# Attention and routed experts in one kernel: where some VectorE copies, two groups of ranking products, and the stores of eight pairs of output rows are placed

## The chip, the cores and the metric

The kernel runs on one core of a Trainium2 chip. The metric is the device time of one execution in microseconds; the time before is the median of three runs. The engines are named as in the profile: PE (TensorE, with PEld for its weight loads), DVE (VectorE), ACT (ScalarE), POOL (GpSimd) and SP (SyncE, which here only issues DMAs). Each engine carries out its own instructions in the order of the program; engines wait for each other by semaphores.

## What is computed

Linear attention without a softmax, a normalization of each head's rows, and on the result a layer of eight experts of which each row uses one:

```python
q, k, v: (8, 8, 576, 64)                       # batch, heads, rows, head dim
kv  = einsum('bhsd,bhse->bhde', k, v)
out = einsum('bhsd,bhde->bhse', q, kv)
x   = out / sqrt(mean(out*out, -1) + 1e-6) * g_norm     # then (4608, 512): heads side by side
compute = x @ w_skip > 0                       # the other rows are returned as they are
logits  = x @ w_gate                           # 8 experts
e       = argmax(logits);  gate = softmax(logits)[e]
y       = gate * (relu(x @ w1[e]) @ w2[e])     # w1: (8, 512, 1024), w2: (8, 1024, 512)
out     = x + y
```

## The kernel before

All matrices are 32-bit floats. The order of all work is written out by hand: the program is one schedule, and what stands earlier in it for an engine runs earlier on that engine.

**Attention** goes over 36 *units*. A batch has 9 rows for each of 64 partitions; a *pair* `nq` is a tile `xb` of 128 partitions by 2 rows by 512 columns (512 KB) of final x, and two units (four heads each, `u` = 0 and 1) make one pair. Every batch has two pairs (`i` = 0, 1: eight of its nine rows), and after each four batches comes one pair with the ninth rows (`i` is None). So pairs 0 to 7 are of batches 0 to 3, pair 8 their ninth rows, 9 to 16 of batches 4 to 7, pair 17 the rest. `starts[b]` is the first unit of batch b: 0, 4, 8, 12, 18, 22, 26, 30; units 16 and 17 are pair 8, units 34 and 35 pair 17.

For a batch, `state` (L383) sums k^T v in PSUM (`sum_ps`), ScalarE copies it to SBUF (`both`, L390), and from there it goes into a block matrix `kvd`: DVE copies the halves that change partitions (`other`, L394), POOL those that stay (`own`, L395). `state_t` (L400) transposes it, and `state_m` (L408) multiplies the router's weights into it, whose result ScalarE copies into the 9 columns at the ends of `kvd` by four small copies (L412). `kvT_ps`, the router's products and the rank table lie in one PSUM bank, the tile `g_ps`. A batch's `state` work is cut into pieces and put into the steps of the batch before (`portions`).

**Steps.** The schedule's main loop has one step for each unit n. On PE and ACT a step holds, in this order: `turn(n+1)`, the transposes of q (L460) and the copy `qT` (L463, ACT); the square root of unit n-1 (L529, ACT); jobs of the part "early"; `values(n)`, the products q·kvd (L498, or L508 for ninth rows) in one of two PSUM buffers, with the ninth rows' transposes (L479) in the first units of a batch, and the squares on ACT (L514); jobs of "mid"; on DVE the sums of squares (L522) and the normalization of unit n-1 (reciprocal L536, `xl` L545, which sets the PSUM buffer free); jobs of "pe"; POOL's sums of logits (L597 to L605); and jobs of "end". POOL multiplies by g_norm one step later (`xb`, L615), held back until DVE's reciprocal.

**Gating** has three groups (`ends = [12, 22, 36]`). For the first two, a generator hands DVE a few small instructions at the end of each step (2 a step for group 0, 4 for group 1): the chosen expert by maximum and comparison (`choose`, L665 to L685, one-hot `ohb`), then `rank` on PE (L696, L699, L702), which counts the rows in front of each row for its expert, then `number` on DVE. `rank` runs in step 16 for group 0 and in step 24 for group 1, in the part "pe", behind the `state_m` that runs in the same step. Behind group 1 the experts are sorted by their number of rows, SP reads the order into registers and loads the first expert's `w1` (L337, step 26). From the known rows (batches 0 to 4) the first expert's first rows are then looked up (`early`, L899 to L915, with PE's L924) and gathered from the output in DRAM by POOL (L917, step 30). PE turns them at L848 in step 33, and the first layer on them starts at L859.

**DMA.** SP issues all loads of q, k and v (L118; k and v have three buffers, q two, and the load of batch b + 2 of q stands at the end of step `starts[b] + 2`), the weights, and most stores of x. A finished pair is stored by two halves of 256 KB: at the end of the step that follows its last multiplication on POOL, not before `store_from` (step 24 for pairs 8 and 9). For pairs with i = 1 of batches 0 to 6, POOL issues the first half itself (L649), SP the second (L653). `xb` has six buffers. The pool `wpool_a` holds one expert's `w1` and `w2`; the room of `w2` is used from the start for the router's rows, a few constants and a block of zeros (`room`), the room of `w1` stands empty until L337. `load_second` loads `w2` in step 32.

**Filling products.** `dense` issues products of a constant with itself, 128x512 in bf16 (L171), whose result nobody reads; they stand where PE would wait at the start, and once near the end of attention.

Behind the attention come the eight experts, one by one, with weights in two pools in turn (L1172, L1184, L1252 on PE; results scattered by POOL at L1383).

Of the kernel before, what the change touches and what calls it, by code (L numbers as in the profile page):

```python
# [8 lines left out]
FP32 = mybir.dt.float32  # L9
# [8 lines left out]
def kernel(  # L18
# [43 lines left out]
    nc = tc.nc  # L62
    B, H, S, D = q.shape
    DM = H * D
    N = B * S
    P = 128
# [6 lines left out]
    E, F = moe_w1.shape[0], moe_w1.shape[2]  # L73
    G = E + 1
    KD = D + G
    DC = DM // 128
# [71 lines left out]

    room = wpool_a.tile([P, FC, DM], FP32, tag="w2", name="w2")
    room = room[:, :, :].rearrange("p c d -> p (c d)")  # L150
    wrow = room[0:4, 0:P * E].rearrange("p (q n) -> p q n", n=E)
    nc.scalar.dma_start(out=wrow, in_=moe_w_gate.rearrange("(j q) n -> j q n", q=P))
    srow4 = room[0:4, P * E:P * G]
# [11 lines left out]

    warm_ps = ps_q.tile([P, 512], FP32, tag="q", name="q_ps")

    def dense(count, ps=warm_ps):

        for _ in range(count):  # L170
            nc.tensor.matmul(out=ps[:, :], lhsT=ones[:, :],  # L171
                             rhs=ones[:, :].unsqueeze(1).to_broadcast([P, 4, P]), start=True, stop=True)

    dense(11)

# [39 lines left out]
    for n in range(G):  # L215
# [3 lines left out]
    gcol_ps = set_ps[:, 1, 0:1]  # L219
    nc.tensor.transpose(out=gcol_ps, in_=room[0:1, P * G:P * G + 2 * D],  # L220
                        identity=ident[0:1, 0:1])
    dense(2)
    gcol = setup.tile([P, 1], FP32)
    nc.scalar.copy(out=gcol[:, :], in_=gcol_ps)
    gbig = room[:, P * G + P:P * G + 2 * P]
# [125 lines left out]
            tc.add_manual_dep(ins.ins, behind.ins.name, WAIT, reason="gathers first")  # L351


    kvTs, boths = {}, {}

    def own(b, w):

# [2 lines left out]
    def other(b, w):  # L360

        return kvds[b % KVD][(1 - w) * 64:(2 - w) * 64, w, 1 - w, :, :]
# [12 lines left out]
    def state(b, some):  # L375

        kt, vt = kts[b], vts[b]
        for i in some:
            u, c = divmod(i, C)
            for w in range(2):  # L380
                for a in range(2):
                    r = slice(a * 64, (a + 1) * 64)
                    nc.tensor.matmul(  # L383
                        out=sum_ps[w * 64:(w + 1) * 64, a, u, :],
                        lhsT=kt[r, 2 * u + w, c, :], rhs=vt[r, 2 * u + w, c, :],
                        start=(c == 0), stop=(c == C - 1), skip_group_check=True)
        if some.stop < 2 * C:
            return
        both = att_pool.tile([P, 2, 2 * D], FP32, tag="both", name="both", bufs=1)
        nc.scalar.copy(out=both[:, :, :].rearrange("p u (a d) -> p a u d", a=2), in_=sum_ps)  # L390
        boths[b] = both
        cols = slice(G, G + 2 * D)
        for w in range(2):
            nc.vector.tensor_copy(out=other(b, w)[:, :, cols], in_=both[w * 64:(w + 1) * 64, :, :])  # L394
            nc.gpsimd.tensor_copy(out=own(b, w)[:, :, cols], in_=both[w * 64:(w + 1) * 64, :, :])  # L395

    def state_t(b):
        both = boths.pop(b)
        for u in range(2):
            nc.tensor.transpose(out=kvT_ps[:, u, :], in_=both[:, u, :], identity=ident[:, :])  # L400
        kvT = att_pool.tile([P, 2, P], FP32, tag="kvT", name="kvT", bufs=1)
        nc.scalar.copy(out=kvT[:, :, :], in_=kvT_ps)
        kvTs[b] = kvT

    def state_m(b):
        kvT = kvTs.pop(b)
        for u in range(2):
            nc.tensor.matmul(out=lg_ps[:, u, :, :, :], lhsT=kvT[:, u, :], rhs=gw_b[:, u, :, :, :],  # L408
                             start=True, stop=True)
        for w in range(2):  # L410
            for to in (own, other):
                nc.scalar.copy(out=ends_of(to(b, w)), in_=lg_ps[w * 64:(w + 1) * 64, :, :, w, :])  # L412


    units = []
    nq = 0
# [25 lines left out]
    def at(step, part, job):  # L442
        todo.setdefault((step, part), []).append(job)
# [165 lines left out]
    def weigh(n, xl):  # L609

        nq, b, i, u = units[n]
        if u == 0:
            xbs[nq] = xb_pool.tile([P, 2, DM], FP32, tag="xb", name="xb")
        xb = xbs[nq]
        late.append((lambda eng: eng.tensor_tensor(  # L615
            out=xb[:, :, 4 * u * D:(4 * u + 4) * D].rearrange("p r (w x) -> p r w x", w=2),
            in0=xl[:, :, :, G:G + 2 * D] if i is None else
            xl[:, :, :, G:G + 2 * D].rearrange("p w r x -> p r w x"),
            in1=g_b[:, :, :].rearrange("p a d -> p (a d)").unsqueeze(1).unsqueeze(1)
                .to_broadcast([P, 2, 2, 2 * D]), op=ALU.mult), nq, u == 1 and (lambda: store_x(nq, b, i))))  # L620

    store_from = {x[0]: starts[B - 3] + 2 for x in units if x[1:3] in ((0, None), (4, 0))}

    def scale(n, behind=None, keep=0, eng=None):

# [9 lines left out]
    def store_x(nq, b, i):  # L635

        xb = xbs.pop(nq)
        if i is None:
            rows = out.rearrange("(f hf r p c) d -> f hf p r c d", f=NF, hf=2, r=2, c=C)[b]
            def store():  # L640
                for hf in range(2):
                    nc.sync.dma_start(out=rows[hf, :, :, C - 1, :], in_=xb[hf * 64:(hf + 1) * 64, :, :])
            return store
        rows = out[b * S:(b + 1) * S, :].rearrange("(p c) d -> p c d", c=C)[:, 4 * i:4 * i + 4, :]
        rows = rows.rearrange("p (hf r) d -> hf p (r d)", hf=2)
        x = xb[:, :, :].rearrange("p r d -> p (r d)")
        first = int(i == 1 and b < B - 1)
        if first:
            nc.gpsimd.dma_start(out=rows[0], in_=x[0:64, :])  # L649

        def store():
            for hf in range(first, 2):
                nc.sync.dma_start(out=rows[hf], in_=x[hf * 64:(hf + 1) * 64, :])  # L653
        return store
# [295 lines left out]
            in_=zero)  # L950

    state(0, range(C))
    dense(4)
    state(0, range(C, 2 * C))
    dense(2)
    state_t(0)
    turn(0)
    state_m(0)
# [5 lines left out]
    for b, n in starts.items():  # L964
        if b:
            step, counts = portions[b]
            i = 0
            for count in counts:
                at(step, "early" if step in (starts[2], starts[4] - 2) else "pe",
                   lambda b=b, some=range(i, i + count): state(b, some))  # L970
                i += count
                step += 1
            assert i == 2 * C and step < n and step - len(counts) > over - 1
            at(step, "early", lambda b=b: state_t(b))
            at(step, "pe", lambda b=b: state_m(b))
            over = step
        at(over, "end", lambda b=b: load_kv(b + 3, range(4 if b > 1 else 2)))

        at(n + 2, "end", lambda b=b: load_q(b + 2))
        if b < 2:  # L980
            at(n + 2, "end", lambda b=b: load_kv(b + 3, range(2, 4)))

    def gating(g):

        yield from choose(g)
        yield lambda: rank(g)
        numbers = number(g)
        yield next(numbers)
        if g == LAST - 1:
            yield from rank_experts()  # L990
            load_weights(0, wpool_a, later=True)
        yield from numbers
        if g == LAST - 1:
            yield from early()
# [633 lines left out]
```

## Time and profile before

| | |
|---|---|
| runs | 366.98, 367.38, 367.67 us; median 367.38 |
| profiled execution | 366.29 us, of which the span of instructions 364.4 us |
| granted PE clock, mean | 0.994 |
| busy | PE 349.5, PEld 305.5, DVE 249.2, ACT 145.1, POOL 125.7 us |
| moved by DMA | 81.70 MB, mean 224 GB/s |

In the profile, times are microseconds from the first instruction. "PE g_ps L696 x2" is two instructions of line 696 that write the tile g_ps; what stands in brackets behind an instruction is how long its engine was idle before it, and what ended the wait. The chain is followed back from the last instruction, at each step to what released it. A float32 product appears as two passes, so 16 products of L508 are 32 instructions.

### The profile page before, as it was taken

Reading aid. Unit: us, or ns where it says so; the run is one execution under the profiler, and the core shown is the slowest. Engines: PE = TensorE matmul, PEld = TensorE weight load, DVE = VectorE, ACT = ScalarE, POOL = GpSimd, SP = SyncE. Lnnn points to the kernel's source line nnn. Section 1 sums busy time; section 2 is a strip of 40 time slices with the busy share of each in tenths; the row PEclk is TensorE's granted clock in tenths of the full one; section 3 lists DMA queues with packets and bytes.
Section 4 is the critical chain, followed back from the end, with each engine's and each line's share of the span. In section 5 each row is a group of like instructions: output and inputs, shape, how many; then the busy total and the mean of one; then the engine's idle time right before and its main releaser. Section 6 shows DMA issues by size and latency. Waiting matters only on the chain.

```text
span 364.4 us, 9568 instructions
## 1 busy us (share of the span) xinstructions
PE 349.5 (96%) x3754; PEld 305.5 (84%) x3754; DVE 249.2 (68%) x637; ACT 145.1 (40%) x418; POOL 125.7 (34%) x205
## 2 busy tenths in 40 slices
PE   8979998999899999999999999999999999999994
PEld 4769987888779669599879978989988998989983
DVE  2545677889888563876937676786776776878831
ACT  2537775676666244244104402512421530431420
POOL 8036777677776072123041102303203203002003
PEclk9989999999999999999999999999999999999999
DMA  8999999999797369873535537455563762601001
GB/s 272 387 390 377 371 392 398 394 394 384 247 335 255 104 208 379 340 262 89 209 107 205 171 124 254 121 224 176 175 230 98 250 235 53 243 1 58 3 2 54
DMA packets 32808, 81.70 MB, mean 224 GB/s; under 512 B 3242, under 2 KB 3250, under 8 KB 32756
## 3 DMA queue, kind: packets, MB, share of 16 engines
q1 hardware_dynamic: 28944, 69.48, 53.7%
q0 software_dynamic: 3792, 11.53, 9.3%
q8 instruction: 31, 0.51, 0.5%
q14 instruction: 21, 0.17, 0.1%
q10 hardware_dynamic: 20, 0.02, 0.0%
HBM read 66.80 MB, written 14.48 MB: 223 GB/s over the span
## 4 chain that ended last, share of the span: by engine, by line
PE 79%; issue 6%; DMA 5%; DVE 5%; POOL 2%; ACT 2%; SPq 0%; POOLq 0%; DVEq 0%; ACTq 0%
PE bank L1252 46%; PE bank L1184 9%; PE o_ps L498 6%; PE sum_ps L383 4%; PE bank L1172 3%; PE q_ps L460 3%; DMA v<-in_v_dram 2%; PE bank L1153 2%; DVE xl L545 1%; DMA xg<-out_dram,src 1%; PE g_ps L859 1%; DMA xg<-out_dram,asrc 1%; PE q_ps L859 1%; PE o_ps L479 1%; DVE rs L522 1%
## 5 line engine op out<-in xcount | busy, mean ns | idle before, releaser
L1262 ACT COPY p<-bank 128x128 f32<-128x128 f32 (+6 forms) x70 | 20.8, 297 | 96.1 <-PE bank L1252 94.6
L1252 PE MATMUL bank<-xt,w 128*128 128x128 f32 (+5 forms) x336 | 55.4, 288 | 0.1
L1383 POOL DMA_INDIRECT out_dram<-xg,rows x14 | 13.9, 996 | 116.2 <-DVE xg L1380 113.0
L1252 PEld LDWEIGHTS bank<-xt,w 128*128 128x128 f32 x336 | 47.0, 190 | 1.9 <-DVE bank L1256 1.4
L615 POOL TENSOR_TENSOR xb<-xl,g_b 128x512 f32<-128x512 f32 x34 | 41.3, 1216 | 18.1 <-DVE rs L536 16.1
L1256 DVE TENSOR_TENSOR bank<-bank,p 128x128 f32<-128x128 f32 (+6 forms) x70 | 23.6, 337 | 29.7 <-PE bank L1252 28.7
L498 PE MATMUL o_ps<-kvd,qT 128*128 128x146 f32 x240 | 36.0, 293 | 1.3 <-DVE xl L545 1.0
L1252 PE MATMUL bank<-xs,s 128*128 128x128 f32 (+5 forms) x224 | 36.7, 288 | 0.0
L498 PEld LDWEIGHTS o_ps<-kvd,qT 128*128 128x128 f32 x240 | 32.1, 192 | 2.1 <-DVE xl L545 1.8
L1252 PEld LDWEIGHTS bank<-xs,s 128*128 128x128 f32 x224 | 31.1, 190 | 1.0 <-ACT p L1262 0.8
L1184 PE MATMUL bank<-w,ht 128*32 128x128 f32 (+2 forms) x424 | 29.9, 313 | 0.0
L522 DVE TENSOR_REDUCE rs<-sq 128x8 f32<-128x512 f32 x36 | 24.5, 681 | 5.4 <-ACT sq L514 5.2
L545 DVE TENSOR_TENSOR xl<-o_ps,rs 128x584 f32<-128x584 f32 x32 | 24.5, 767 | 4.3 <-DVE rs L536 0.5
L1184 PEld LDWEIGHTS bank<-w,ht 128*32 128x32 f32 (+2 forms) x424 | 18.2, 119 | 10.6 <-issue 7.2
L1252 PE MATMUL bank<-t,ht 128*128 128x256 f32 x112 | 27.0, 384 | 0.0
L1252 PE MATMUL bank<-w,ht 128*128 128x256 f32 x112 | 26.5, 380 | 0.0
L383 PE MATMUL sum_ps<-v,k 64*64 64x64 f32 x1152 | 23.5, 223 | 3.0 <-issue 2.6
L1144 POOL DMA_INDIRECT xg<-out_dram,src x14 | 14.3, 1024 | 34.8 <-DMA out_dram<-xg,rows 18.0
L514 ACT ACTIVATE sq<-o_ps 128x512 f32<-128x512 f32 x34 | 20.3, 596 | 14.1 <-PE o_ps L498 13.2
L383 PEld LDWEIGHTS sum_ps<-v,k 64*64 64x64 f32 x1152 | 19.6, 134 | 7.1 <-issue 3.9
L1252 PE MATMUL bank<-t,hs 128*128 128x256 f32 x112 | 25.3, 379 | 0.0
L1252 PEld LDWEIGHTS bank<-t,ht 128*128 128x128 f32 x112 | 20.8, 190 | 3.9 <-issue 1.2
(216 smaller groups left out, 665.2 us busy)
## 6 DMA issues: line engine op xcount, KB each, us to landing
w<-in_moe_w_dram SPq DMA_DIRECT2D x16, 2048.0 KB, 9.0
k<-in_k_dram SPq DMA_DIRECT2D x32, 288.0 KB, 6.0
v<-in_v_dram SPq DMA_DIRECT2D x32, 288.0 KB, 6.3
q<-in_q_dram SPq DMA_DIRECT2D x32, 288.0 KB, 6.2
out_dram<-xb SPq DMA_DIRECT2D x29, 256.0 KB, 6.1
out_dram<-xb POOLq DMA_DIRECT2D x7, 256.0 KB, 6.4
xg<-out_dram,src POOLq DMA_INDIRECT x16, 3.6
out_dram<-xg,rows POOLq DMA_INDIRECT x16, 6.1
```

The source lines that it names most:

```text
L383: nc.tensor.matmul(out=sum_ps[w * 64:(w + 1) * 64, a, u, :], lhsT=kt[r, 2 * u + w, c, :], rhs=vt[r, 2 * u + w, c, :], start=(c == 0), stop ...
L498: mm = nc.tensor.matmul(out=ps[:, w, 0:2 * PK].rearrange("p (r k) -> p r k", r=2)[:, :, cols], lhsT=qT[:, w, a, :], rhs=kvds[b % KVD][:, w ...
L514: nc.scalar.activation(out=sq[:, :, :, :], in_=heads(ps, G, G + 2 * D), func=ACT.Square)
L522: nc.vector.tensor_reduce(out=rs[:, :, :], in_=sq[:, :, :, :].rearrange("p x y (a d) -> p x (y a) d", a=2), axis=AX.X, op=ALU.add)
L545: nc.vector.tensor_tensor(out=xl[:, :, :, :].rearrange("p x y (a k) -> p x (y a) k", a=2), in0=ps[:, :, 0:2 * PK].rearrange("p x (h k) -> ...
L615: late.append((lambda eng: eng.tensor_tensor(out=xb[:, :, 4 * u * D:(4 * u + 4) * D].rearrange("p r (w x) -> p r w x", w=2), in0=xl[:, :, ...
L1144: nc.gpsimd.indirect_dma_start(out=x_of(xg, off, m), out_offset=None, in_=cut_rows(m)[:, :], in_offset=bass.IndirectOffsetOnAxis(ap=idx[:, ...
L1184: nc.tensor.matmul(out=yps[q * m:(q + 1) * m, 0:n], lhsT=ht(f)[:, off:off + m], rhs=w_sb[r][1][:, f, q * n:(q + 1) * n], start=(f == 0), s ...
L1252: nc.tensor.matmul(out=out, lhsT=lhsT(i), rhs=rhs(i), start=start and i == 0, stop=i == k - 1, skip_group_check=True)
L1256: nc.vector.tensor_tensor(out=to, in0=x, in1=y, op=ALU.add)
L1262: nc.scalar.copy(out=t, in_=x)
L1383: ins = nc.gpsimd.indirect_dma_start(out=cut_rows(m)[:, :], out_offset=bass.IndirectOffsetOnAxis(ap=rows[:, col:col + 1], axis=0), in_=x, ...
```

## The change

- `held` takes the empty room of the first expert's `w1`. Pairs 2 to 5 of x are written into it, pairs 6 to 9 into the room of its `w2`; pairs 0, 1 and from 10 on use the buffers of `xb`.
- Pairs 0 to 10 are stored from given steps on: 2 and 3 from step 20, 4 and 5 from 21, 6 from 22, 0, 1, 7, 8 and 9 from 24 (behind the load of q of batch 7, which stands at the end of the same step), 10 from 25. Both halves of these are issued by SP, so five of POOL's seven issues (L649) are gone.
- For batches 5, 6 and 7 the two copies to `other` are made by ScalarE in the step before the batch's first unit (steps 21, 25 and 29), in "mid", that is behind that step's squares.
- `rank` of groups 0 and 1 moves from "pe" to "mid": on PE it comes right behind the step's `values`, ahead of `state_m` and of the piece of `state` in "pe".
- Three runs of filling products at the start are issued as four times as many of 128 columns.

```diff
+    held = wpool_a.tile([P, DC, F], FP32, tag="w1", name="w1")
+    held = held[:, :, :].rearrange("p c f -> p (c f)")
...
-    def dense(count, ps=warm_ps):
-
-        for _ in range(count):
-            nc.tensor.matmul(out=ps[:, :], lhsT=ones[:, :],
-                             rhs=ones[:, :].unsqueeze(1).to_broadcast([P, 4, P]), start=True, stop=True)
+    def dense(count, ps=warm_ps, cut=1):
+
+        for _ in range(count * cut):
+            nc.tensor.matmul(out=ps[:, 0:512 // cut], lhsT=ones[:, :],
+                             rhs=ones[:, :].unsqueeze(1).to_broadcast([P, 4 // cut, P]),
+                             start=True, stop=True)
...
-    dense(2)
+    dense(2, cut=4)
...
-    kvTs, boths = {}, {}
+    kvTs, boths, ACROSS = {}, {}, 5
...
         for w in range(2):
-            nc.vector.tensor_copy(out=other(b, w)[:, :, cols], in_=both[w * 64:(w + 1) * 64, :, :])
+            if b < ACROSS:
+                nc.vector.tensor_copy(out=other(b, w)[:, :, cols], in_=both[w * 64:(w + 1) * 64, :, :])
             nc.gpsimd.tensor_copy(out=own(b, w)[:, :, cols], in_=both[w * 64:(w + 1) * 64, :, :])
 
+    def state_across(b):
+        if b < ACROSS:
+            return
+        both = boths.pop(b)
+        for w in range(2):
+            nc.scalar.copy(out=other(b, w)[:, :, G:G + 2 * D], in_=both[w * 64:(w + 1) * 64, :, :])
+
     def state_t(b):
-        both = boths.pop(b)
+        both = boths[b]
...
         if u == 0:
-            xbs[nq] = xb_pool.tile([P, 2, DM], FP32, tag="xb", name="xb")
+            home = nq - ROOMS_FROM
+            if 0 <= home < 8:
+                x = (held, room)[home // 4][:, home % 4 * 2 * DM:(home % 4 + 1) * 2 * DM]
+                xbs[nq] = x.rearrange("p (r d) -> p r d", r=2)
+            else:
+                xbs[nq] = xb_pool.tile([P, 2, DM], FP32, tag="xb", name="xb")
...
-    store_from = {x[0]: starts[B - 3] + 2 for x in units if x[1:3] in ((0, None), (4, 0))}
+    ROOMS_FROM = 2
+    at_q7 = starts[B - 2] - 2
+    store_from = {0: at_q7, 1: at_q7, 2: at_q7 - 4, 3: at_q7 - 4, 4: at_q7 - 3, 5: at_q7 - 3,
+                  6: at_q7 - 2, 7: at_q7, 8: at_q7, 9: at_q7, 10: at_q7 + 1}
...
-        first = int(i == 1 and b < B - 1)
+        first = int(i == 1 and b < B - 1 and nq not in store_from)
...
     state(0, range(C))
-    dense(4)
+    dense(4, cut=4)
     state(0, range(C, 2 * C))
-    dense(2)
+    dense(2, cut=4)
...
             at(step, "pe", lambda b=b: state_m(b))
+            at(n - 1, "mid", lambda b=b: state_across(b))
...
         yield from choose(g)
-        yield lambda: rank(g)
+        yield "mid", lambda: rank(g)
```

## The prediction

> **What bounds the kernel now.** I read the page first, then the busy time of each engine in stretches of ten microseconds, the chain of work that ended last, the timelines of PE, DVE, ACT and SP around the lines of the diff, and last the DMA. All edits act before 107 us; what follows (the experts) is PE work end to end, so I take a shift of the first gathered rows as a shift of the end.
>
> ```profile
> span 364.4 us, 9568 instructions
> ...
> PE   8979998999899999999999999999999999999994
> ```
>
> ```profile
> 70.00:80.00 10.00, 10.00 (x188) 8.95 (x182) 8.42 (x20) 6.93 (x20) 6.95 (x14) 1.00 1.03 392
> 80.00:90.00 10.00, 9.34 (x203) 8.43 (x204) 9.15 (x28) 6.62 (x18) 6.91 (x12) 1.00 1.04 383
> 90.00:100.00 10.00, 8.33 (x108) 7.51 (x107) 8.99 (x25) 6.56 (x20) 7.85 (x16) 1.00 0.76 261
> ```
>
> The columns are the stretch, its length, then busy time of PE, PEld, DVE, ACT and POOL, the granted clock, the DMA share and GB/s. From 70 to 80 us PE has no gap: attention runs at PE's pace. From 80 to 100 PE loses 0.66 + 1.67 = 2.3 us while DVE is 18.1 of 20 us busy: there the second gating group's work is threaded between the units on DVE, and DVE sets the pace. DMA is full until 90 us. The chain names the two places where the ranking products sit, and the road to the first gather:
>
> ```profile
> 61.81 0.20 ACT kvd L412
> 62.05 0.47 PE g_ps L696 x2
> 62.57 0.34 PE g_ps L702 x12
> 62.90 0.51 PE q_ps L460 x4
> 63.44 0.58 ACT qT L463
> ...
> 65.38 0.41 PE o_ps L479 x2
> ...
> 82.01 0.29 DVE kvd L394
> 82.33 0.41 DVE kvd L394
> ...
> 83.13 0.49 DVE ohb L685
> ...
> 84.40 0.46 PE g_ps L696 x2
> ...
> 85.14 0.49 PE q_ps L460 x4
> ...
> 93.04 0.29 DVE kvd L394
> 93.36 0.37 DVE kvd L394
> ...
> 99.75 0.71 PE g_ps L924 x22
> ...
> 101.37 5.18 DMA xg<-out_dram,src
> 106.69 0.63 PE q_ps L848 x4
> ```
>
> Start, length, and what. The first product of `rank` (L696) starts right behind ScalarE's small copies out of the same PSUM bank (61.81 + 0.20, then 62.05). Two pairs of `kvd` copies on DVE (L394) lie on the chain. The gather lands 0.14 us before PE uses it (101.37 + 5.18 = 106.55), so whatever brings the gather forward brings the rest forward only if PE, too, comes earlier; both hang on the same DVE chain.
>
> **The change part by part.** *Ranks first, group 0 (step 16).* The unit's products run before L408; the order of PE there is
>
> ```profile
> 59.84 0.69 PE L508 MATMUL o_ps<-kvd,q 64*64 64x73 f32 x32
> 60.46 0.64 PE L408 MATMUL g_ps<-gw_b,kvT 128*128 128x36 f32 x4
> ```
>
> and the one-hot that `rank` reads is done before that:
>
> ```profile
> 60.23 0.27 DVE L685 TENSOR_TENSOR ohb<-eorder,fi 128x96 bf16<-128x96 f32 x1
> ```
>
> So in "mid", ahead of L408, `rank` waits for nothing: it starts at about 60.6 and lasts as now, 62.90 - 62.05 = 0.85, to 61.45; L408's 0.45 follows to 61.9, and PE's next transposes start at 61.9 instead of 62.90, 1.0 earlier. But ScalarE's four copies (0.8 in all, they start when L408 has ended) now run 61.95 to 62.75 and stand ahead of the qT copy, which so moves from 63.44 to 62.8. From there the chain above is kept: qT, root, reciprocal, xl, and PE's L479 at 64.75 instead of 65.38. **-0.6**, between 0 (the wait turns up behind L412 again) and -1.0 (all that PE gains).
>
> *Ranks first and the copies of batch 6 (step 24).* Here the one-hot is late: it ends at 83.62, while the unit's products end at 82.79:
>
> ```profile
> 81.80 1.16 PE L498 MATMUL o_ps<-kvd,qT 128*128 128x146 f32 x8
> 82.79 0.53 PE L408 MATMUL g_ps<-gw_b,kvT 128*128 128x36 f32 x4
> 83.25 0.69 PE L383 MATMUL sum_ps<-v,k 64*64 64x64 f32 x32
> ```
>
> The edit alone would make PE wait in front of L408 and L383, which stand behind it: 83.65 + 0.74 (rank, 85.14 - 84.40) + 0.46 + 0.62 = 85.47, 0.3 later than 85.14. But the DVE copies of batch 6 (82.01 to 82.74) go to ScalarE, so the one-hot ends near 82.9, and PE comes out at 82.95 + 1.82 = 84.77. **-0.4**, between +0.3 (one-hot no earlier) and -0.6 (no wait left).
>
> *The copies of batch 7 (step 28).* DVE has 0.72 us less to do at 93.04 (start of the first copy to 93.76, the next instruction), with no idle time of its own behind it until the gather's index is built. PE waits for DVE there:
>
> ```profile
> 96.19 1.26 PE L498 MATMUL o_ps<-kvd,qT 128*128 128x146 f32 x8 [1.02 <-DVE xl L545]
> 97.29 0.60 PE L460 MATMUL q_ps<-ident,q 128*128 128x128 f32 x4
> ...
> 97.94 1.16 PE L498 MATMUL sum_ps<-kvd,qT 128*128 128x146 f32 x8
> 99.75 0.69 PE L924 MATMUL g_ps<-bv,oha_k 128*128 128x4 bf16 x22 [0.65 <-DVE bv L904]
> ```
>
> Taken from 96.19 and from 99.75, both DVE's: **-0.7**, between 0 and -1.0 (the whole wait). The copies of batch 5 lie where PE is full, between 70 and 80: 0.
>
> *What ScalarE takes over.* Two copies of 64x256 for each of batches 5 to 7, in steps 21, 25 and 29, right before the unit that reads them. The trace has no such copy from SBUF; the nearest rows are
>
> ```profile
> 81.09 0.37 ACT L390 COPY both<-sum_ps 128x256 f32<-128x256 f32 x1
> 97.55 0.60 ACT L514 ACTIVATE sq<-o_ps 128x512 f32<-128x512 f32 x1 [0.48 <-PE o_ps L498]
> ```
>
> 0.37 each, 0.74 the pair. They stand behind the squares (0.60, of which I take 0.5, since the next instruction overlaps its end), so the next unit's products can start 1.25 to 1.3 after the last ones end. In steps 21 and 25 PE has a piece of state (0.62, as at 83.25) and transposes (97.94 - 97.29 = 0.65) in between, 1.27: just covered. What waits on ScalarE is the next qT copy and the root behind it, some 0.1 late in step 21, where they lead to the gating group's first maximum: **+0.1**. In step 29 only the 0.65 lies between, so unit 30 starts 0.6 late; but L924, behind it on PE, has 0.65 of slack. If the units move up by 1.1 (0.4 + 0.7), unit 30 ends near 98.5 and L924's operand comes at 98.6: nothing lost. Without that cover: up to +0.6. The Trainium skill ("ScalarE: Activation LUTs", Rules for kernel authors) speaks against such a move: simple element work belongs on VectorE. In this trace DVE's copies have no better price:
>
> ```profile
> L394 DVE COPY kvd<-both x16: 286/372/452, 12.5 to 93.4; 64x256 f32<-64x256 f32 x16
> ```
>
> median 372 ns against 372 for L390, and from 80 to 100 us ACT is two thirds busy where DVE is nine tenths. By that page's own price (186 ns + 0.833 an element, an estimate of 399 ns) the pair would be 0.80 and the sum 0.1 worse.
>
> *Stores.* Pairs 0 to 10 (0.52 MB each, as the page's 256 KB a half says) are no longer stored as they come but from step 20 on, wholly by SP. SP's queue now:
>
> ```profile
> 78.02 6.06 SPq L118 DMA_DIRECT2D q<-in_q_dram  x8
> ...
> 92.71 0.42 SPq L337 DMA_DIRECT2D w<-in_moe_w_dram  x1
> ```
>
> ```profile
> 90.00:92.00 2.00, 2.00 (x44) 1.85 (x46) 1.66 (x7) 1.09 (x4) 1.50 (x5) 1.00 0.82 324
> 92.00:94.00 2.00, 2.00 (x37) 1.75 (x30) 1.91 (x6) 1.85 (x6) 1.70 (x3) 1.00 0.20 43
> ```
>
> The last loads (q of batches 6 and 7) are issued at 78 to 84, behind stores; afterwards they get ahead by the eight pairs' time (4.2 MB at 390 GB/s, 10.8 us, less where buffers hold them). The same bytes have to land before the gather. I lay them out: q6 leaves at about 70 us (step 20, by the unit's place between 65.38 and 81.80), ten store halves follow (2.6 MB, 6.7 us, to 81.3), q7 leaves when its buffer is free at about 80 and lands by 84.5, and twelve halves behind it (3.1 MB, 8.1 us) land by 92.5; today the DMA drains near 91.6 (0.82 of the stretch from 90 to 92, then 0.20). The gather leaves near 100, so 7 us of slack remain: **0**, and +1 at the worst from traffic shared with the gather. The load of `w1` waits for the stores out of its room, which lie ahead of it on the same queue, and today leaves at 92.71, 14 us ahead of L848. What the earlier loads are good for: q6, issued from 78.02 on, feeds the transposes at 85.14, and would soon stop the gain above. POOL loses five L649 issues:
>
> ```profile
> L649 POOL DMA_DIRECT2D out_dram<-xb x7: 579/582/612, 34.1 to 106.6; - x7
> ```
>
> 0.58 each; from 70 to 100 us POOL is busy 7 of 10 and waits for DVE: 0, at best -0.3, half of one.
>
> *Short products.* Three runs of 512-column products become four times as many of 128 columns. Products of a few dozen columns already cost in proportion to their columns (L702: 12 products of 96 to 8 columns, 52 in the mean, in 0.34 us, 28 ns each, so some 70 ns for 128; four make 0.28, a 512-column one 0.27 by the chain's row below).
>
> ```profile
> 12.09 0.54 PE q_ps L171 x2
> ```
>
> They fill waits for loads and for a ScalarE copy of the 0.37 above, which ends near 12.5, when they do: **0**, -0.1 to +0.1. The Trainium skill ("TensorE: Matmul & The Clock Gate", Back-to-back issue gap) gives 81 ns for a sustained 128-column product with its weight load; by that, an estimate, the eight in that place would take 0.65 instead of 0.54 and the sum would be 0.1 worse. No row here has this shape.
>
> The sum: -0.6 - 0.4 - 0.7 + 0.1 = **-1.6 us**. The profiled execution took 366.29 us (364.4 span, 1.9 around it): 364.7. The median of the three runs is 367.38, 1.1 above that execution; taken from it: **365.8**.
>
> **The rivals.** *PE or ACT takes over (about the same).* The DVE copies are gone, but from 80 to 90 PE loses only 0.66 us, and DVE's 9.15 of 10 there is hardly less than PE's 9.34. If the units from 25 on stay at PE's pace and the index is held by ScalarE's roots, only one of the three gains comes through: -0.4 to -0.7, 366.8. For it: 100% busy PE from 70 to 80. Against: the 1.02 and 0.65 us waits for DVE at the end.
>
> *ScalarE's copies hold the units (slower).* The next unit reads the far halves that DVE wrote 4 us ahead (93.04 for 97.94); afterwards they come behind the squares of the unit before. If a copy from SBUF costs twice the 0.37, the pair lasts 1.48 and the products wait 1.98 after the unit before, against 1.27 of cover: 0.7 in step 21, 0.7 in step 25, and in step 29 1.98 - 0.65 - 0.65 = 0.7, which eats batch 7's gain. The sum is +2.1 against -0.6, -0.4 and what is left of -0.7: about +0.8, 368.2. It decides from a copy of about 0.6 us up. For: the copies stand in a strict order on ACT and PE behind them. Against: L390's 0.37.
>
> *More than forecast.* PE's own waits vanish whole (-1.0, -0.6, -1.0) and POOL's 0.3 comes too: -2.9, 364.5. *The edit does nothing.* If L408 is held by DVE's reading of the rank bank, the wait has only moved: 0 at step 16, and the whole is -0.5.
>
> **How the numbers follow.** Forecast (-0.8 to -2.4) 0.52; more 0.10; takeover or no effect 0.24, of which a quarter is still beyond 0.2%; slower 0.14. A difference of 0.2% is 0.73 us, about what a measurement of this kernel can tell from none. Faster: 0.52 + 0.10 + 0.06 = 0.68; same 0.18; slower 0.14. The range leaves out a tenth on each side: down to -3.2 (every upper bound and 0.3 for the base), 364.2, and up to +0.6, 368.0, nearly as far as the slower rival.
>
> **What would show it.** L696 with no wait for L412 at the first place and under 0.2 us at the second; L479 of step 18 some 0.6 earlier; two ACT copies of 0.37 in each of three steps; PE's wait for xl at unit 29 below 0.3; L924 near 98.2 and L848 near 105.1; the DMA drained by 93, no wait of the gather on a store. I am wrong if ACT's copies pass 0.6, if L498 of unit 30 waits over 1 us, if the gather takes over 6 us to land, or if the shift is there at L848 and gone at the end.

## The result and the profile after

The kernel after the change takes 371.06 us (median of 4 runs, 369.94 to 371.4), the kernel before 367.52 beside it (4 runs): a ratio of 1.0096, 95% interval 1.0075 to 1.0118. The change is slower by about 3.5 us. The profiled execution took 369.94 us with a span of 368.1; before, 366.29 and 364.4.

From the page of the kernel after (span, and PE's busy tenths):

```profile
span 368.1 us, 9615 instructions
...
PE   8979998999859999999999999999999999999993
```

There is one new hole in PE's row, the 5 from 101 to 110 us (slices of 9.2 us). By stretches of ten microseconds (PE, PEld, DVE, ACT, POOL, granted clock, DMA share, GB/s):

```profile
70.00:80.00 10.00, 10.00 (x201) 9.15 (x201) 7.50 (x19) 7.76 (x21) 6.63 (x13) 1.00 0.85 280
80.00:90.00 10.00, 9.79 (x172) 8.74 (x171) 8.74 (x27) 7.40 (x21) 7.06 (x13) 1.00 0.91 292
90.00:100.00 10.00, 8.93 (x120) 7.85 (x119) 8.67 (x24) 7.59 (x22) 7.90 (x13) 1.00 0.86 297
100.00:110.00 10.00, 6.06 (x60) 4.84 (x63) 6.53 (x15) 4.44 (x11) 7.99 (x14) 0.93 0.77 258
```

Up to 100 us PE is busier than before (9.79 for 9.34, 8.93 for 8.33), so the compute edits act. The DMA moves 280 and 292 GB/s where it moved 392 and 383, and is still busy behind 92 us (share 0.86 from 90 to 100, 0.76 before). Then PE loses 3.9 of 10 us. The timeline of PE shows both halves (a bracket is the idle time before, and who ended it; L715 is `rank`'s first product, L943 makes the gather's index, L867 turns the first gathered rows, L878 is the first layer):

```profile
60.38 0.47 PE L715 MATMUL g_ps<-top,ident 128*128 128x104 f32 x2
...
64.59 0.41 PE L490 MATMUL o_ps<-ident,q 128*64 128x128 f32 x2 [0.65 <-DVE xl L556]
...
82.09 0.46 PE L715 MATMUL g_ps<-top,ident 128*128 128x88 f32 x2
...
94.35 1.26 PE L509 MATMUL o_ps<-kvd,qT 128*128 128x146 f32 x8 [0.21 <-DVE xl L556]
...
96.88 1.23 PE L509 MATMUL sum_ps<-kvd,qT 128*128 128x146 f32 x8 [0.61 <-ACT kvd L406]
98.05 0.69 PE L943 MATMUL g_ps<-bv,oha_k 128*128 128x4 bf16 x22
...
108.42 0.93 PE L867 MATMUL q_ps<-ident,xg 128*128 128x128 f32 x4 [3.62 <-DMA xg<-out_dram,src]
109.28 1.25 PE L519 MATMUL o_ps<-kvd,q 64*64 64x73 f32 x32
...
113.12 2.46 PE L878 MATMUL g_ps<-xt_first,w 128*128 128x64 f32 x16
```

In the kernel before, the ninth rows' products (L519 there is L508) and the first layer's were:

```profile
107.25 0.74 PE L508 MATMUL o_ps<-kvd,q 64*64 64x73 f32 x32
...
109.92 2.46 PE L859 MATMUL g_ps<-xt_first,w 128*128 128x64 f32 x16
```

The index products are 1.70 us earlier than before (99.75). The gathered rows' first product is 1.73 us later (106.69), after a wait of 3.62 us; the sixteen products of the first layer are 3.20 later (109.92), because PE's work after the wait costs more: L519 takes 1.25 us where the same work before took 0.74. The span ends 3.7 later, so 3.2 of these have arisen by 113 us, all of them behind 100. The queue of SP says where from (start, time from the first to the last of a run of issues):

```profile
70.13 2.74 SPq L118 DMA_DIRECT2D q<-in_q_dram  x4
72.97 9.12 SPq L672 DMA_DIRECT2D out_dram<-w  x10
82.18 2.71 SPq L118 DMA_DIRECT2D q<-in_q_dram  x4
84.93 3.46 SPq L672 DMA_DIRECT2D out_dram<-xb  x4
...
95.14 2.04 SPq L672 DMA_DIRECT2D out_dram<-xb  x2
101.02 0.42 SPq L340 DMA_DIRECT2D w<-in_moe_w_dram  x1
```

Ten store halves take 9.12 us, 0.91 each. Pair 10's halves, which the gather has to wait for, are issued at 95.14, and `w1`, 2 MB, leaves at 101.02 (before: 92.71). The chain of work that ended last then runs through the gather:

```profile
96.33 0.41 ACT kvd L406
...
100.93 7.36 DMA xg<-out_dram,src
...
108.42 0.93 PE q_ps L867 x4
```

It leaves 0.4 us earlier than before, not 1.7, and takes 7.36 us instead of 5.18.

### The profile page after: what moved, and what is told of

It is laid out like the page before. It is cut to its first block, busy times and chain, and to the rows that moved or that the text cites. A ratio compares the mean times of both kernels' runs of the same rounds, so it can differ in the third digit from the quotient of the medians.

```text
span 368.1 us, 9615 instructions
## 1 busy us (share of the span) xinstructions
PE 351.8 (96%) x3778; PEld 307.8 (84%) x3778; DVE 247.0 (67%) x631; ACT 147.7 (40%) x424; POOL 124.0 (34%) x200
## 4 chain that ended last, share of the span: by engine, by line
PE 72%; DMA 11%; issue 7%; DVE 5%; ACT 1%; SPq 1%; POOL 1%; POOLq 0%; DVEq 0%; ACTq 0%
PE bank L1272 45%; PE bank L1204 7%; DMA v<-in_v_dram 6%; PE o_ps L509 4%; PE sum_ps L386 3%; PE bank L1192 2%; PE q_ps L471 2%; DMA xg<-out_dram,src 2%; PE bank L1173 2%; PE q_ps L173 2%; DMA q<-in_q_dram 2%; DMA out_dram<-xb 1%; DVE oha_k L747 1%; SPq L118 1%; DMA xg<-out_dram,asrc 1%
## 5 line engine op out<-in xcount | busy, mean ns | idle before, releaser
L631 POOL TENSOR_TENSOR xb<-xl,g_b 128x512 f32<-128x512 f32 x18 | 22.3, 1239 | 14.8 <-DVE rs L547 11.0
```

The costliest lines, as they stand in the source:

```text
L631: late.append((lambda eng: eng.tensor_tensor(out=xb[:, :, 4 * u * D:(4 * u + 4) * D].rearrange("p r (w x) -> p r w x", w=2), in0=xl[:, :, ...
```

## The experiments

All ratios are against runs of the kernel before on the same chip (their medians lay between 367.3 and 370.2 us), with a 95% interval.

**One half of the change at a time.** The first run undoes `held`, the rooms, `store_from` and the edit to `first`; the second does these alone.

```diff
-            home = nq - ROOMS_FROM
-            if 0 <= home < 8:
-                x = (held, room)[home // 4][:, home % 4 * 2 * DM:(home % 4 + 1) * 2 * DM]
-                xbs[nq] = x.rearrange("p (r d) -> p r d", r=2)
-            else:
-                xbs[nq] = xb_pool.tile([P, 2, DM], FP32, tag="xb", name="xb")
+            xbs[nq] = xb_pool.tile([P, 2, DM], FP32, tag="xb", name="xb")
...
-    store_from = {0: at_q7, 1: at_q7, 2: at_q7 - 4, 3: at_q7 - 4, 4: at_q7 - 3, 5: at_q7 - 3,
-                  6: at_q7 - 2, 7: at_q7, 8: at_q7, 9: at_q7, 10: at_q7 + 1}
+    store_from = {x[0]: starts[B - 3] + 2 for x in units if x[1:3] in ((0, None), (4, 0))}
```

> The change without its rooms and store times: ranks first, ScalarE's copies for batches 5 to 7 and the short products stay; pairs are stored as before. Theory A (the late burst of stores makes the loss: SP and the DMA are held by it, the first expert's w1 leaves 8 us late and runs into the first gather, which itself waits for pair 10): the -1.6 us of the forecast come out, 365.5 to 366.3, with L848's counterpart near 105. Theory B (the moved copies and ranks make the loss, the burst only shows it): 368 or more.

> The kernel before with the rooms and the store times alone. Theory A: w1 leaves at about 101 us as in the changed kernel, the gather takes over 7 us to land, and the end comes at 370.5 to 371.5, about the time of the whole change, since both are then set by SP and the DMA and not by DVE. Theory B: 367 to 368.

Without the store moves: 0.9995 (0.9976 to 1.0015), no difference. With the store moves alone: 1.0162 (1.0129 to 1.0194); ten halves take 9.78 us, `w1` leaves at 101.48 and PE waits 2.55 us for the gather. So the loss is the stores', as the first theory has it. But the compute edits by themselves gain nothing, which that theory did not have. PE's timeline of the first run has waits that the kernel before does not have:

```profile
60.70 0.44 PE L469 MATMUL q_ps<-ident,q 128*128 128x128 f32 x2 [0.30 <-DMA q<-in_q_dram]
...
72.82 0.41 PE L469 MATMUL q_ps<-ident,q 128*128 128x128 f32 x2 [0.60 <-DMA q<-in_q_dram]
...
107.30 0.63 PE L857 MATMUL q_ps<-ident,xg 128*128 128x128 f32 x4 [1.18 <-DMA xg<-out_dram,src]
```

PE comes sooner and finds the q's not there; its index products start at 99.37, only 0.38 earlier than before, and the gather is late for PE all the same.

**Spreading the stores, and filling the wait.** The third run issues the store halves from step 17 on; the fourth leaves the stores as changed and puts fourteen idle products ahead of the gathered rows.

```diff
+    store_from = {0: at_q7 - 2, 1: at_q7 - 2, 2: at_q7 - 7, 3: at_q7 - 7, 4: at_q7 - 6, 5: at_q7 - 6,
+                  6: at_q7 - 5, 7: at_q7 - 5, 8: at_q7 - 3, 9: at_q7 - 1, 10: at_q7 + 1}
```

> The changed kernel with the same rooms, but the stores spread: pairs 2 and 3 from step 17, 4 and 5 from 18, 6 and 7 from 19, 8 from 21, 0 and 1 from 22, 9 from 23, 10 from 25. Theory A: the DMA's gap at 68 to 73 us is filled, w1 leaves before 96 us, the gather lands within 6 us: 365.5 to 367. Theory C (x in the weights' rooms, not the time of its stores, is what costs): 370 or more.

```diff
+    at(NU - 3, "pe", lambda: dense(14, ps_q.tile([P, 512], FP32, tag="q", name="q_ps")))
```

> The changed kernel with 14 more filling products of 512 columns (3.6 us) right in front of the first turning of gathered rows, where PE waits 3.6 us. Does the wait cost only itself, or also the clock that is granted behind it (0.65 and 0.5 from 108 to 112 us)? If the clock: the products behind it run at full rate again and 1.0 to 1.7 us come back, 369.4 to 370.1. If not: 370.8 to 371.3.

The third: 1.0091 (1.0056 to 1.0126), no better than the change; twelve halves now stand ahead of a q that PE waits 1.57 us for at 84.15. This would fit the rival of that run too, that x in the weights' rooms is what costs; a schedule below with the same rooms, at 0.9999, speaks against it. The fourth: 1.0015 (0.9991 to 1.0039). Both were run again beside each other, the change as it is and with the filling:

> The changed kernel itself, on the same chip as the next two, so that they have something to stand beside: 1.005 to 1.015 of the kernel before, first gather 7 us or more under way, PE's wait in front of the turning above 2 us.

> The changed kernel with 14 filling products in front of the first turning, as before, beside the changed kernel on the same chip. If PE's wait costs the clock behind it too, it is 1.0 to 2.5 us faster than the changed kernel there and the products behind the wait run at full rate; if the wait costs only itself: within 0.5 us of it.

1.0083 (1.005 to 1.0115) and 1.0014 (0.9986 to 1.0042): filled with idle work, the wait gives back 0.7%. This is read from the medians of 9 and 12 runs; single executions differ too much. The change, run twice, and the change with the filling, run twice, are the same program up to the filling, and in their four profiles `w1` leaves at 101.02, 100.51, 99.50 and 97.97 us and the gathered rows land at 108.3, 109.9, 107.2 and 105.4. The change as it is, by stretches of two microseconds behind its wait of 6.20 us there:

```profile
106.00:108.00 2.00, 0.00 (x0) 0.00 (x0) 0.22 (x1) 0.00 (x0) 1.68 (x4) 0.89 0.97 264
108.00:110.00 2.00, 0.00 (x1) 0.03 (x1) 0.00 (x0) 0.00 (x0) 1.84 (x5) 0.50 0.97 350
110.00:112.00 2.00, 2.00 (x36) 1.67 (x36) 0.00 (x0) 0.79 (x2) 1.14 (x2) 0.50 1.03 418
112.00:114.00 2.00, 2.00 (x21) 1.85 (x14) 0.84 (x3) 1.16 (x3) 0.10 (x1) 0.50 1.02 384
```

The granted clock falls to 0.50 and stays there for 4 us of work. With the filling it is 1.00 from 106 to 112 us (0.57 and 0.58 from 98 to 102, with PE busy all the time and no wait ahead of it over 0.61; why is not known). So part of the loss is not the wait but the clock after it; how much, these executions don't tell apart. The Trainium skill ("TensorE: Matmul & The Clock Gate", What's actually happening) has the clock halved after an idle window of about 3.4 us; the 3.62 and 6.20 us here agree, and a case below does not.

**What a store half costs by itself.** A kernel that computes nothing of the reference and only stores and loads.

> Measures the disputed price by itself and computes nothing of the reference (constant rows are stored): stores of half a pair as in the kernel (64 partitions by 4 KB, the two halves of SBUF's partitions in turn), then all from partitions 0 to 63, then whole 128-partition stores of 512 KB, then halves issued by SP and ACT in turn, then halves and loads of 288 KB in turn, then loads alone; between the groups SP waits for all to land. If stores alone are slow whatever their shape: 250 to 290 GB/s in the first four groups, 380 or more in the last two. If only the 64 partitions of a half are slow: the whole stores move at 350 or more. If one queue is the limit: the group on two queues moves at 350 or more. By the forecast's price all groups move at 390.

Halves taken from the lower and upper 64 partitions in turn (L78, 32 of them), halves from the lower 64 alone (L82, 24), and stores of twice the size from all 128 partitions (L85, 12):

```profile
7.05 29.98 SPq L78 DMA_DIRECT2D out_dram<-x  x32
43.49 28.56 SPq L82 DMA_DIRECT2D out_dram<-x  x24
80.38 13.47 SPq L85 DMA_DIRECT2D out_dram<-x  x12
```

From the first issue to the last that is 0.94 us a half, 1.19 from one side alone, and 1.12 for one of the double size. In the middle of the three runs the DMA moves 298, 230 and 396 GB/s, of which a small read-back of what was stored is a part; SP's queue alone moves 272, 209 and 370. At 370 a store of the double size takes 1.42 us and not 1.12: the last ones are still under way when the issuing ends. The prediction's 0.67 a half is near the rate of the wide kind. The wide stores also go to unbroken rows of the output, which the halves don't, so partitions and rows are not told apart here. Three more groups follow in that run: halves issued by SP and ScalarE in turn move 344 GB/s (106 to 116 us), halves from the lower side and loads in turn 309 with the read-back (132 to 150), loads alone 392 (162 to 170). So a half is no cheaper among loads, and one queue for all the halves may be a part of the price; the group on two queues did not reach the 350 that was to decide this.

**Stores among the loads.** An earlier schedule for the stores, then the same with the first halves of pairs 1, 3, 5, 7 and 10 back on GpSimd's queue, then with eight idle products as well:

```diff
+    store_from = {0: 10, 1: 12, 2: 14, 3: 16, 4: 17, 5: 20, 6: 20, 7: 20, 8: 24, 9: 24, 10: 24}
-        first = int(i == 1 and b < B - 1 and nq not in store_from)
+        first = int(i == 1 and b < B - 1)
+    at(NU - 3, "pe", lambda: dense(8, ps_q.tile([P, 512], FP32, tag="q", name="q_ps")))
```

> The changed kernel, its stores put between the loads and not behind them: pair 0 from step 10, 1 from 12, 2 from 14, 3 from 16, 4 from 17, 5 to 7 from 20 (behind q of batch 6), 8 to 10 from 24 (behind q of batch 7). Same bytes, same rooms. If what costs is that stores in a row move slower than stores among loads and that SP, in order, comes late to w1 with them: SP is through its stores by 90 us, w1 leaves by 94, the gather takes under 6 us, and the forecast's -1 to -2 us against the kernel before come out (0.994 to 0.998). If the rooms, ScalarE's copies or the ranks were to blame: 1.005 or more, as the change.

> The change with its stores spread among the loads from step 10 on (as in the third schedule), and with the gathered sequence's first halves given back to GpSimd's queue, as before the change. Theory (a row of store halves moves slowly and keeps SP from w1): SP has five halves of 0.9 us less, reaches w1 at 93 to 95 us, w1 has landed when the gather leaves near 98, the gather takes 5 to 6 us, PE's wait for it is under 1 us, and the time is 0.993 to 0.998 of before. Rival (the loads, not w1, eat the gain, or GpSimd's issues give it back): w1 early all the same, but the index products no earlier than 99.5 us, ratio 0.998 to 1.003.

> As the run beside it (stores among the loads, first halves on GpSimd's queue), with eight idle products of 512 columns more ahead of the first gathered rows. If the gather lands in time there, PE has little to fill: within 0.5 us of the run beside it, or up to 1 us slower. If PE still waits over 1.5 us for the gather and its clock falls, this one is 1 to 3 us faster.

0.9999 (0.9971 to 1.0027), 1.0011 (0.9987 to 1.0035) and 0.9992 (0.9965 to 1.002). The loss is gone, but no gain comes where the first two were expected at 0.993 to 0.998, though the index is now far ahead: 96.12, 97.68 and 96.75 us for 99.75 before. The second of them on PE, and by stretches:

```profile
97.68 0.69 PE L942 MATMUL g_ps<-bv,oha_k 128*128 128x4 bf16 x22
...
106.84 1.09 PE L866 MATMUL q_ps<-ident,xg 128*128 128x128 f32 x4 [2.41 <-DMA xg<-out_dram,src]
```

```profile
106.00:108.00 2.00, 1.16 (x8) 0.86 (x12) 0.77 (x1) 0.04 (x1) 1.84 (x5) 0.60 1.03 416
108.00:110.00 2.00, 2.00 (x37) 1.86 (x38) 0.13 (x1) 1.51 (x4) 0.74 (x2) 0.50 1.03 409
```

The gather left at 99.3 and landed at 106.7: the index comes sooner, the rows do not. Here the clock halves after an idle time of 2.41 us, shorter than the window that the Trainium skill names. The length alone doesn't decide it: in the run with the stores from step 17 a longer wait left the work behind it at its full speed (granted clock 1.00 from 110 to 112 us):

```profile
109.64 0.63 PE L867 MATMUL q_ps<-ident,xg 128*128 128x128 f32 x4 [2.66 <-DMA xg<-out_dram,src]
```

The theory of these runs, that `w1` must only leave before the gather, was then tried by itself.

**`w1` sooner, `w1` later.** SP read all eight expert numbers before it issued `w1` (in the kernel after the first at 97.2 and the last at 100.5); now it reads one, issues `w1`, and reads the others behind it. The fourth run is the same edit on the kernel before; the one called late moves `w1` behind the index in the program.

```diff
         for r in range(E):
             experts_of.append(nc.values_load(
                 order_i[0:1, r:r + 1], engines=(mybir.EngineType.SP,), min_val=0, max_val=E - 1,
                 skip_runtime_bounds_check_because="a permutation of the experts"))
+            if r == 0:
+                load_weights(0, wpool_a, later=True)
```

> The kernel before with one thing moved: the load of the first expert's w1 is issued behind the index for the gather instead of ahead of the last gating group's work, so it leaves at 99 to 102 us, as in the changed kernel, without any store moved. Theory (w1 beside the gather is a large part of the loss): the gather lands in over 6.5 us instead of 5.2, PE waits 1.5 to 2.5 us for it, the clock falls, ratio 1.004 to 1.010. Rival (only the store that the gather waits for counts, w1 is harmless): within 0.2% of before.

> The change with its stores among the loads and the first halves on GpSimd's queue (as in the first of the x runs), and one thing more: SP reads the first expert's number alone, issues w1, and reads the other seven numbers behind it, so w1 leaves some 3 us sooner with nothing else moved. Theory (w1 beside the gather eats what the compute edits win): w1 leaves at 92 to 94 us instead of 96.5, the gather takes 5 to 6 us instead of 7.4, PE's wait falls from 2.4 us to under 1, the clock stays whole, and the ratio is 0.991 to 0.997. Rival (the gather's length has another cause, such as its rows or the stores): it still takes over 7 us and the ratio stays at 1.00.

> As the run beside it, with the eight idle products ahead of the gathered rows. Theory: with the gather in time there is nothing to fill, so this one is 0 to 1.5 us slower than the run beside it, at 0.994 to 1.0 of before. Rival (the gather is late all the same): this one is 1 to 3 us faster than the run beside it.

> The change as it is, with w1 issued behind the first expert's number alone: it leaves at 97.5 to 98.5 us instead of 101.0. Theory: the gather still waits for pair 10's store to about 100.9 and then shares the DMA engines with w1, which is only half done: it takes 6 to 7 us instead of 7.4, and the ratio falls from 1.008 to 1.003 to 1.007. Rival (only the store counts): no change, 1.008.

> Control: the kernel before with the same edit to w1 alone. w1 leaves near 89.6 us instead of 92.7, and has landed well before the gather leaves at 101.4 in either case. Theory: the gather at 5 to 5.2 us as now, ratio 0.998 to 1.002. Rival (w1's leaving sooner is a gain by itself, for the products that read it): under 0.997.

The late one missed its aim: SP runs ahead, and `w1` left at 94.45, 1.7 us later than before. The gather took 6.53 us, PE waited 1.53, the ratio is 1.006 (1.0035 to 1.0085); a right sign on a shift that was not the one wanted. `w1` first in the spread schedule: 0.9972 (0.9936 to 1.0007), and with filling 0.9969 (0.9937 to 1.0). On the change as it is: 1.0007 (0.9974 to 1.004), better than expected, although the execution that was profiled still waited 4.24 us, for a gather of 7.84. The control: 0.9988 (0.9954 to 1.0022). Its gather took 2.9 us where 5 to 5.2 were expected: SP's queue thinned out by 104 us, the rows moved from then on, and PE, busy with attention until 107.4, did not wait for them. So `w1`'s late issue cost the change about 0.8% (1.0083 and 1.0007, on two chips); the profile of that run doesn't show how. And the first of these four contradicts its own theory: `w1` left 1.9 us sooner (94.57 for 96.49), and the gather took 7.91 us instead of 7.4. The DMA by queue from 99 to 103 us of that run shows why (q1 is SP's queue, q0 would be GpSimd's; packets, MB, share of the engines):

```profile
DMA packets 313, 1.24 MB, mean 309 GB/s; under 512 B 14, under 2 KB 14, under 8 KB 312
...
q1 hardware_dynamic: 312, 1.22, 96.2%
```

The gather left at 98.58, and in the four microseconds from 99 on GpSimd's queue moves no packet at all. Microsecond by microsecond its rows, 0.39 MB, move from 103.9 to 106.5, when SP's queue thins out. How soon the rows can move is seen where SP's queue has nothing to do: in the last control below (gather issued at 101.92) the first of them move 1.7 us after the issue, and they land 2.9 us after it. So here some 3 us were lost. The kernel before, from 100 to 104 us, with its gather issued at 101.37, loses about 1 us in the same way; its rows begin at 104.0:

```profile
q1 hardware_dynamic: 478, 1.64, 102.0%
...
q0 software_dynamic: 1, 0.00, 0.0%
```

**Bytes taken out of SP's queue.** Between `w1` and `w2` SP issues five store halves, 1.3 MB, of pairs 11 to 13, which the first gather does not read. The next two runs are the spread schedule with the halves back and `w1` first, and move all five, or three of them, behind `w2`'s issue; the last makes the same two queue edits (`w1` first, five halves behind) on the kernel before.

```diff
-                  6: 20, 7: 20, 8: 24, 9: 24, 10: 24}
+                  6: 20, 7: 20, 8: 24, 9: 24, 10: 24,
+                  11: NU - 3, 12: NU - 3, 13: NU - 3}
```

> As the run with w1 first (stores among the loads, first halves on GpSimd's queue, SP reading one expert's number ahead of w1), and the five store halves of pairs 11 to 13, which the first gather does not read and which SP issues between w1 and w2, moved behind w2's issue. Theory now (the gather's rows on GpSimd's queue move only when what SP has queued ahead of them is through: w1's 2 MB and five halves, 1.3 MB): with 1.3 MB or 3 to 4 us less ahead, the gather issued at 98.6 us moves its rows at 101 to 102 instead of 104 and lands by 104 instead of 106.5, PE's wait falls from 2.9 us to under 1, and the ratio is 0.990 to 0.996, unless pair 17, whose buffer is pair 11's, gives it back at the end of attention. Rival (the gather is slow by itself, whatever is queued): it lands at 106 to 107 as before.

> The same with only the three halves of pairs 12 and 13 moved, so that no later pair waits for a buffer. Theory: 0.8 MB or 2 us less ahead of the gather: rows from 102 us, landed by 105, PE's wait 1 to 2 us, ratio 0.993 to 0.998. Rival: as the run beside it, 106 to 107 and no gain over the run with w1 first (0.997).

> Control to the run with pairs 11 to 13 behind w2: the kernel before, its short products, ranks, copies, rooms and stores as they were, with only w1 first and the five halves of pairs 11 to 13 moved behind w2's issue. Theory (two things must come together: an index that is ready early, and a queue without bytes ahead of the gather): the gather still leaves near 101.4 us, lands by 104 to 105 instead of 106.6, and PE, whose own work runs to 106.6, starts on it only 0.1 to 0.3 earlier; ratio 0.998 to 1.001. Rival (the bytes behind w2 are the whole gain): 0.990 to 0.995, as there.

All five: 0.9919 (0.989 to 0.9949), 364.84 us against 367.26, faster than both kernels. Its SP queue, its DMA from 99 to 103 us, and PE:

```profile
91.89 0.42 SPq L340 DMA_DIRECT2D w<-in_moe_w_dram  x1
100.77 0.39 SPq L350 DMA_DIRECT2D w<-in_moe_w_dram  x1
102.85 8.36 SPq L672 DMA_DIRECT2D out_dram<-xb  x8
```

```profile
q0 software_dynamic: 128, 0.39, 37.2%
q1 hardware_dynamic: 160, 0.40, 34.1%
```

```profile
96.27 0.69 PE L945 MATMUL g_ps<-bv,oha_k 128*128 128x4 bf16 x22
...
102.85 0.60 PE L869 MATMUL q_ps<-ident,xg 128*128 128x128 f32 x4
```

Now 128 packets, all of the gather, move in the stretch in which the run before moved none. They land before PE is done with attention; L869 has no wait and stands 3.84 us ahead of the kernel before, and the span is 3.8 shorter (360.6). That execution, at 362.37 us, is the fastest of its six; the medians are 2.4 us apart. Three halves: 0.997 (0.9939 to 1.0001), 48 packets in that stretch, rows landed at 106.0 and 2.21 us of wait. The rows are in between, but the time is that of the run with `w1` first (0.9972), as the rival of this run had it. On the kernel before: 1.0001 (0.9975 to 1.0027). There SP's queue is empty from 101 to 105.5 us and the rows come in time, but PE is not ready for them:

```profile
105.79 1.26 PE L498 MATMUL sum_ps<-kvd,qT 128*128 128x146 f32 x8
106.89 0.60 PE L851 MATMUL q_ps<-ident,xg 128*128 128x128 f32 x4
```

So neither the queue's order alone nor an earlier index alone is worth anything that shows; together they are worth 0.8%. That the rows wait while SP's queue is full is measured; what makes them wait is not. Left open: which of the change's edits that run needs, since the rooms and the compute edits were not taken apart in it; and stores of whole pairs from 128 partitions in place of halves, which were not tried.

## Why the prediction was wrong

*The compute steps held.* Ranks first: L490 at 64.59 for 65.38, -0.79 where -0.6 was forecast, with no wait at either place. The copies: 0.41 us on ScalarE for the 0.37 taken; PE's wait for xl at unit 29 is 0.21 (forecast under 0.3), unit 30 waits 0.61 for ScalarE and the index products behind it wait for nothing. They start at 98.05, near the 98.2 forecast. The rivals' conditions did not come: the index is 1.70 us earlier, so PE did not take over, and ScalarE's copies stay under the 0.6 us from which they would have cost; the 0.61 at unit 30 is what the forecast itself had. The short products cost nothing either way, eight of 128 columns 0.62 us where two of 512 took 0.61.

*The step that failed is "Stores": "so 7 us of slack remain: 0, and +1 at the worst".* It failed in two of its terms. First the price: "ten store halves follow (2.6 MB, 6.7 us, to 81.3)" costs a half at 390 GB/s, which is what the DMA moved from 70 to 90 us in the kernel before. A row of halves takes 0.91 us each in the kernel and 0.94 by itself, 0.67 by that price. The twenty-two halves that were to have landed by 92.5 are issued until 97.2, and then SP still has to read eight numbers (97.2 to 100.5) before `w1`. Then what the slack was measured against: it was counted to the last store, with the load of `w1` "14 us ahead" of its use. But `w1`'s 2 MB go through the same DMA engines as the gather, and here the gather's rows did not move before them. `w1` at 101.02 meets the gather at 100.93 and, though issued 0.09 us behind it, moves first: SP's queue alone moves from 102 to 105.9, the rows from 105.9 to 108.3, 5.0 us after their issue where 1.7 is enough with an empty queue. The wait for pair 10's store (2.2 us on GpSimd) comes on top: the gather leaves 2.88 us behind the index products, before 1.62. PE's 3.62 us of waiting cost 1.5 more in the work behind it, at a granted clock of 0.65 and 0.50 from 108 to 112 us, so the shift of the first rows (1.7) was not the shift of the end (3.7), as the forecast took it to be. The runs that bear this out: the store moves alone lose 1.6%, `w1` 3.5 us sooner brings the change back to 1.0007, and filling the wait to 1.0014.

*A second step failed that would have cost the forecast even without the stores.* The 5.18 us of the row "101.37 5.18 DMA xg<-out_dram,src" were read as the gather's own duration, so that a shift of the index became a shift of the rows. With little in SP's queue it is 2.9 us (in both controls on the kernel before). In the kernel before, too, the rows moved only from 104.0 on, when SP's queue thinned out, and in five of these kernels (the one before, the two with the halves back on GpSimd's queue, and the same two with `w1` first) they landed between 106.3 and 106.7 for an index anywhere from 96.75 to 99.75. That the loads of q would "soon stop the gain" with the stores in their old places, the prediction had said itself: without the store moves 1.3 of the 1.7 us are lost to waits for loads before the index, and the rest at the gather (0.9995). The sum of -1.6 was right at the index, and there was no way for it to reach PE. With the bytes out of the way, an index 3.5 us early (96.27) became rows and an end 3.8 us early in the profiled execution.

The prediction's own test, "if the gather takes over 6 us to land", is what caught it. Its range ended at 368.0, too low by 3; the traffic shared with the gather had been given +1 without a row that bounds it, where `w1`'s 2 MB at the 390 GB/s used there would have said some 5 us.

## What to carry to other kernels

The time from a gather's issue to its landing is not its duration: look by queue at when its packets move, and at what other queues are given before its packets are ready. Ahead of a transfer on which the critical chain hangs, count the bytes that are queued by then, weights included, and move those that nobody needs yet behind it. An edit that makes compute earlier and one that clears the queue can each be worth nothing alone and 0.8% together.

## What the runs showed of the hardware

- A row of 256 KB stores from 64 partitions each takes 0.94 us a store with the sides in turn and 1.19 from one side, 298 and 230 GB/s with a small read-back; stores from 128 partitions, to unbroken rows, move 396. Halves on two queues in turn move 344.
- A gather on GpSimd's queue that was issued at 98.58 us moved no packet from 99 to 103 us, while SP's queue moved 1.22 MB, and 0.39 MB in the same stretch when little was on SP's queue. A gather's first rows moved 1.7 us after the issue with SP's queue empty, 2.6 in the kernel before and 5.0 in the kernel after, there behind a load that was issued 0.09 us later. The Trainium skill ("DMA: Bandwidth & Descriptors", Queues, rings and completion order) has each DMA engine take the queues in turn, packet by packet. The trace differs: by turns the gather would have had a share from about 1.7 us after its issue.
- The clock fell to 0.50 after idle times of PE of 6.20, 3.62 and 2.41 us, and of 2.21 us in the run with three halves moved, and each time the ninth rows' products behind them took 1.25 us for 0.74; after 2.66 us (the stores from step 17) and 1.53 us (the run with `w1` later) it stayed at 1.00.
